# A decode layer's last rows: batch rows 8 partitions apart, and one store for two

## The chip, the cores and the metric

The kernel runs on one core of a Trainium2 chip. The metric is the device time of one execution in microseconds (us), measured on the chip; the median of three runs of the kernel before is 378.41 us (378.24 to 378.53). The profile is of one execution taken by the hardware profiler. PE is TensorE's matmul side and PEld its weight loads, DVE is VectorE, ACT ScalarE, POOL GpSimd, SP SyncE. "SPq" and "ACTq" are the sequencers of those engines, which issue DMAs. L706 is line 706 of the kernel.

## The reference

One layer for one new token in each of four batch rows, D = 576: layernorm, attention over the last 4096 positions of a cache (32 query heads over 16 key/value heads of 128), a projection back to 576, and a feed-forward block with a gated ReLU of width 4608; both with a residual.

```python
def _A_ref(x, k_cache, v_cache, wq, wo):
    W = min(4096, max(256, Sk // 4))                 # Sk = 16384: W = 4096
    q = ((x @ wq).reshape(B, Sq, Hq, Dh)).transpose(0, 2, 1, 3)
    k = jnp.repeat(k_cache[:, :, Sk - W:, :], rep, axis=1)
    v = jnp.repeat(v_cache[:, :, Sk - W:, :], rep, axis=1)
    p = softmax(jnp.einsum("bhqd,bhkd->bhqk", q, k) * (Dh ** -0.5))
    o = jnp.einsum("bhqk,bhkd->bhqd", p, v)
    return o.transpose(0, 2, 1, 3).reshape(B, Sq, Hq * Dh) @ wo

def _B_ref(x, W_gate, W_up, W_down):
    gate = x @ W_gate
    gate = gate * (gate > 0)
    return (gate * (x @ W_up)) @ W_down

h  = x + _A_ref(layernorm(x), k_cache, v_cache, wq, wo)
h2 = h + _B_ref(layernorm(h), W_gate, W_up, W_down)
```

Everything is bf16 in DRAM. The output has 4 rows of 576 values, 4.6 KB. What has to be read is some 160 MB, nearly all of it the K and V windows.

## The kernel before, in words

A small planner (`Prog`) keeps one list of operations for each engine; each names the operations that it depends on. When the lists are written out, each engine waits on the semaphores of what its next operation depends on and then runs it. The order within an engine is the order of the source, and nothing is reordered.

*Loads.* All loads but that of x are issued by SyncE, in one list: wq, then 16 tiles of K and 16 of V of 4 MB each into a ring of four slots (L242), then wo (L266), W_gate and W_up (L276) and W_down in five pieces (L282), cut at rows 0, 15, 25, 32, 35 and 36 of the 36 rows that a partition holds. A load waits only until its place in SBUF has been read for the last time. x is loaded on ScalarE's queue (L335).

*Start.* GpSimd sets the constants (L287 to L329): an identity, masks, zeros. One of them is `sel4`, a 128x32 matrix in fp32 that sums the four groups of 32 partitions into four rows: column b has a one where the partition modulo 32 is b, and the other columns are zero. VectorE finishes some of these constants (L554 to L560), in its list just ahead of the first transposition of K (L422).

*Attention.* For each tile VectorE transposes K in place, PE forms the scores and, four tiles later, the products with V; ScalarE takes the exponentials. This fills the time up to about 340 us.

*Behind attention.* The heads' outputs lie in `oT`, with the four batch rows in columns 0 to 3 of 32. The projection with wo (L607 to L617) runs on the four groups of 32 PE columns side by side, so each group leaves a partial sum of the four rows in the first 4 of its 32 partitions. VectorE and ScalarE copy it out as `part`. Five matmuls (HT, L623; fp32, so PE runs each in two) sum the groups with `sel4` and turn the result round, so that D lies along partitions; residual and layernorm statistics follow (L625 to L643). The normalized rows go to `hnT` (L644, L645), 32 columns per chunk of D, of which columns 0 to 3 hold the batch and the rest are zero.

*Feed-forward.* Gate and up matmuls (L649 to L668) take `hnT` as weights of 32 columns, so that each group of 32 PSUM partitions has the batch in its first 4 rows and zeros in the others. ReLU (L670), product (L673), and a transposition in blocks of 32x32 (L677) give `hhT`, with the batch in columns 0 to 3 of every 32.

*Down projection.* The 576 output columns are cut in two (`ncol`, L681): 272 on PE's columns 0 to 31 and PSUM bank 0, 304 on PE's columns 32 to 63 and bank 1. The two halves of a pass run side by side. Both begin with h: the partial sums `part` through `sel4` (L691), and x through the identity's first 4 rows (L693). 36 passes over W_down's rows follow (L694 to L705); the last has its weights loaded ahead (L697), so only its two matmuls (L34) wait for W_down's last piece.

*Output.* VectorE copies bank 0's half to partitions 0 to 31 of `out_sb` as bf16 (L706), ScalarE bank 1's half to partitions 32 to 63 (L707). The batch rows lie in partitions 0 to 3 and 32 to 35. SyncE stores the first four, ScalarE's queue the second four (L711); both count on the semaphore `d_out`, and SyncE ends by waiting for both (L714, recorded at L110).

Of the kernel before, what the change touches and what calls it, by code (L numbers as in the profile page):

```python
# [6 lines left out]
ALU = mybir.AluOpType  # L7
AX = mybir.AxisListType
FP32 = mybir.dt.float32
BF16 = mybir.dt.bfloat16  # L10

B = 4
# [20 lines left out]
def mm_same(e, out, lhsT, rhs, start, stop, tile, pos):  # L33
    return e.add_instruction(mybir.InstMatmult(  # L34
        name=e.bass.get_next_instruction_name(), engine=mybir.EngineType.PE, ins=[e.lower_ap(rhs), e.lower_ap(lhsT)],
        outs=[e.lower_ap(out)], start_tensor_calc=start, stop_tensor_calc=stop, tile_size=tile, tile_position=pos,
        ldweights=False, bass_skip_group_check=True))
# [83 lines left out]
def bass_sequential_preLN__sliding_block_cached__glu_gated_reglu__decode_kernel(  # L121
# [12 lines left out]
    with ExitStack() as es:  # L134
        cnt = [0]

        def sb(name, shape, dt):
            return es.enter_context(nc.sbuf_tensor("sb_" + name, shape, dt))

        P = Prog()  # L140
        pe = lambda name, fn, deps=(): P.op("tensor", name, fn, deps)
        dve = lambda name, fn, deps=(): P.op("vector", name, fn, deps)
        act = lambda name, fn, deps=(): P.op("scalar", name, fn, deps)
        pool = lambda name, fn, deps=(): P.op("gpsimd", name, fn, deps)
# [6 lines left out]
        ident_b = sb("ident_b", [128, 128], BF16)  # L151
# [6 lines left out]
        c_s4 = o_tmp[:, 512:528].rearrange("p (a b) -> p a b", a=4)  # L158
# [8 lines left out]
        sel4 = sb("sel4", [128, 32], FP32)  # L167
        eps_c = sb("eps_c", [128, 1], FP32)
        warm = sb("warm", [128, 2], FP32)
        x_bf = sb("x_bf", [B, D], BF16)  # L170
# [16 lines left out]
        hnT = sb("hnT", [128, DC + 1, 32], BF16)  # L187
        R_sb = sb("R_sb", [128, DC, 2, B], FP32)
        st2 = sb("st2", [128, 40], FP32)
        tmp5 = sb("tmp5", [128, DC, B], FP32)  # L190
        out_sb = sb("out_sb", [128, 352], BF16)


        pT = pp[:, 0:4096]
# [2 lines left out]
        part = pp[:, 0:1152].bitcast(FP32)  # L197
        partd = pp[:, 1152:1408].bitcast(FP32)
# [7 lines left out]
        bank = [psb[:, i, :] for i in range(8)]  # L206
        bankb = [psb[:, i, :].bitcast(BF16) for i in range(8)]
        ot_ps = bank[6]
        m_ps = bank[7]
# [19 lines left out]
        def ring_slot():  # L229
            s = ring[0] % NSLOT  # L230
            ring[0] += 1
            return s
# [12 lines left out]
        def main_rows(W):  # L245
            return W[0:512, :].rearrange("(p r) n -> p (r n)", r=4)
# [5 lines left out]
        s = ring_slot()  # L252
# [16 lines left out]
        for g, W in ((0, B_W_gate), (1, B_W_up)):  # L269
            for m, n, src in ((4, F // 2, last_rows(W)), (0, 3 * F, main_rows(W)[:, 0:3 * F]), (3, F, main_rows(W)[:, 3 * F:4 * F])):  # L270
                if g == 0 and m == 0:
                    n, src = 4 * F, main_rows(W)
# [7 lines left out]
        for r0, r1 in zip(WD_ROWS, WD_ROWS[1:]):  # L280
            place(("wd", r0), wd_off + r0 * D, (r1 - r0) * D, ("DOWN", 1),
                  lambda e, r0=r0, r1=r1: e.dma_start(  # L282
                      out=arena[:, wd_off + r0 * D:wd_off + r1 * D],
                      in_=B_W_down.rearrange("(p r) n -> p (r n)", p=128)[:, r0 * D:r1 * D]))
# [18 lines left out]
                                                in_=c_qm[:, :, :].rearrange("p q (h j) -> p q h j", j=4),  # L303
# [4 lines left out]
                                                in_=to_v[:, :, :].rearrange("p n (k a) -> p n k a", a=4),  # L308
# [8 lines left out]
        pool("c_s41", lambda e: e.affine_select(out=c_s4[:, :, :], in_=c_s4[:, :, :], pattern=[[-1, 4], [-32, 4]],  # L317
                                                compare_op=ALU.not_equal, fill=1.0, base=0, channel_multiplier=1), ["c_s40"])
        pool("c_sel0", lambda e: e.memset(sel4[:, :], 0.0))
        pool("c_selc0", lambda e: e.memset(selc[:, :, :, :], 0.0))  # L320

        pool("c_toq0", lambda e: e.memset(toq[:, :, :, :], 1.0))
        for sg in range(2):
            pool(f"c_toq{sg + 1}", lambda e, sg=sg: e.affine_select(
                out=toq[:, :, :, :], in_=toq[:, :, :, :],
# [25 lines left out]
        def chunk(t, td, c):  # L351
            return td if c == 4 else t[:, 0:512].rearrange("b (p r) -> b r p", r=4)[:, c, :]
# [186 lines left out]
        def finish_o():  # L539
            for q in range(4):  # L540
                for qd in range(4):
# [11 lines left out]
        put_q()  # L553
        dve("c_qm", lambda e: e.tensor_reduce(out=qm[:, :], in_=c_qm[:, :, :], axis=AX.X, op=ALU.max), ["c_qm1"])  # L554
        dve("c_e8", lambda e: e.tensor_reduce(out=e8[:, :], in_=c_e8[:, :, :], axis=AX.X, op=ALU.max), ["c_e81"])
        dve("c_sel", lambda e: e.tensor_reduce(out=sel4[:, 0:4], in_=c_s4[:, :, :], axis=AX.X, op=ALU.max),
            ["c_s41", "c_sel0"])
        dve("c_selc", lambda e: e.tensor_copy(out=bass.AP(tensor=selc, offset=0, ap=[[128, 128], [33, 4], [4, 8]]),
                                              in_=bass.AP(tensor=e8, offset=0, ap=[[8, 128], [0, 4], [1, 8]])), ["c_e8", "c_selc0"])
        dve("c_toq", lambda e: e.tensor_tensor(out=toq[:, :, :, :], in0=toq[:, :, :, :],  # L560
# [46 lines left out]
        for a in range(8):  # L607
            for n in range(2):
                for j in range(4):
                    out_ = bank[n][32 * j:32 * j + 32, 0:288]  # L610
                    lhsT, rhs = oT[:, 8 * j + a, :], wo[:, 8 * j + a, n * 288:(n + 1) * 288]
                    if n:
                        fn = lambda e, a=a, j=j, out_=out_, lhsT=lhsT, rhs=rhs: mm_same(e, out_, lhsT, rhs, a == 0, a == 7, (128, 32), (0, 32 * j))
                    else:
                        fn = lambda e, a=a, out_=out_, lhsT=lhsT, rhs=rhs: e.matmul(
                            out_, lhsT=lhsT, rhs=rhs, start=(a == 0), stop=(a == 7), skip_group_check=True)
# [3 lines left out]
        dve("partd", lambda e: e.tensor_copy(out=partd.rearrange("p (r a) -> p r a", a=2),  # L620
                                             in_=bass.AP(tensor=psb, offset=512 + 224, ap=[[4096, 128], [1, 64], [0, 2]])), ["part1"])
        for c in range(DC):
            pe("HT", lambda e, c=c: e.matmul(m_ps[:, c * 4:(c + 1) * 4], lhsT=chunk(part, partd, c), rhs=sel4[:, 0:4],  # L623
                                             start=True, stop=True), ["part0", "part1", "partd", "c_sel"] if c == 0 else [])
        dve("h1", lambda e: e.tensor_tensor(out=R_sb[:, :, 0, :], in0=m_ps[:, 0:20].rearrange("p (c b) -> p c b", b=B),  # L625
                                            in1=xT[:, :, :], op=ALU.add), ["HT", "xT"])
# [1 line left out]
        for lo, hi, one in ((0, 4, ones_d), (4, 5, ones_hd)):  # L628
# [4 lines left out]
                                            axis=AX.X, op=ALU.add), ["STAT"])  # L633
# [7 lines left out]
        rstd_bc = bass.AP(tensor=st2, offset=20, ap=[[40, 128], [0, DC], [1, B]])  # L641
        dve("n1", lambda e: e.tensor_tensor(out=tmp5[:, :, :], in0=R_sb[:, :, 0, :], in1=mean_bc, op=ALU.subtract), ["s1"])
        dve("n2a", lambda e: e.tensor_tensor(out=tmp5[:, :, :], in0=tmp5[:, :, :], in1=rstd_bc, op=ALU.mult), ["n1", "s6"])  # L643
        dve("n2", lambda e: e.tensor_copy(out=hnT[:, 0:4, 0:4], in_=tmp5[:, 0:4, :]), ["n2a", "c_hnT"])  # L644
        dve("n3", lambda e: e.tensor_tensor(out=hnT[:, 4:6, 0:4], in0=bass.AP(tensor=tmp5, offset=16, ap=[[20, 128], [0, 2], [1, 4]]),  # L645
                                            in1=bass.AP(tensor=par, offset=0, ap=[[2, 128], [1, 2], [0, 4]]), op=ALU.mult), ["n2a", "c_hnT"])


        for g in range(2):  # L649
            for c in (4, 0, 1, 2, 3):  # L650
                part_ = c if c == 4 or (c == 3 and g) else 0
                for m in range(3):
                    for j in range(4):
# [4 lines left out]
                        lo = gu_off[(g, part_)] + ((c - part_) * F + 1152 * j if c < 4 else 1152 * (j % 2)) + 384 * m  # L658
                        out_, lhsT = bank[3 * g + m][32 * j:32 * j + 32, 0:384], hnT[:, c if c < 4 else 4 + j // 2, :]
# [3 lines left out]
                        else:  # L663
                            fn = lambda e, out_=out_, lhsT=lhsT, lo=lo, c=c: e.matmul(  # L664
                                out_, lhsT=lhsT, rhs=arena[:, lo:lo + 384], start=(c == 4), stop=(c == 3), skip_group_check=True)
# [10 lines left out]
        for i in range(2):  # L676
            dve(("HHT", i), lambda e, i=i: e.transpose(  # L677
                out=hhT[:, 576 * i:576 * i + 576].rearrange("p (r q) -> p r q", q=32),
                in_=bass.AP(tensor=pp, offset=3712 + 18 * i, ap=[[PPW, 128], [1, 18], [36, 32]])), [("HH", m) for m in range(3)])

        ncol = ((0, 272), (272, 576))  # L681

        def down(n, lhsT, w, start, stop, held=False):
            lo, hi = ncol[n]
            out_ = bank[n][32 * n:32 * n + 32, 0:hi - lo]
            if held:
                return lambda e: mm_same(e, out_, lhsT, w[:, lo:hi], start, stop, (128, 32), (0, 32 * n))
            return lambda e: e.matmul(out_, lhsT=lhsT, rhs=w[:, lo:hi], start=start, stop=stop, skip_group_check=True)  # L688
# [1 line left out]
        for n in range(2):  # L690
            pe(None, down(n, sel4[:, :], part, True, False), [("G", 1)])  # L691
        for n in range(2):
            pe(None, down(n, ident_b[0:B, 0:32], x_bf[:, :], False, False))  # L693
        for r in range(36):  # L694
            if r == 35:
                for n in range(2):
# [1 line left out]
            for n in range(2):  # L698
# [4 lines left out]
                    if r % 18 == 0:  # L703
                        deps.append(("HHT", r // 18))
                pe(("DOWN", n), down(n, hhT[:, 32 * r:32 * r + 32], arena[:, wd_off + r * D:wd_off + r * D + D], False, r == 35, r == 35), deps)  # L705
        dve("OUT0", lambda e: e.tensor_copy(out=out_sb[0:32, 0:272], in_=bank[0][0:32, 0:272]), [("DOWN", 0)])  # L706
        act("OUT1", lambda e: e.copy(out=out_sb[32:64, 0:304], in_=bank[1][32:64, 0:304]), [("DOWN", 1)])  # L707
        orow = out.rearrange("b s d -> (b s) d")
        for n in range(2):
            lo, hi = ncol[n]  # L710
            P.dma(("sync", "scalar")[n], ("O", n), lambda e, n=n, lo=lo, hi=hi: e.dma_start(  # L711
                out=orow[:, lo:hi], in_=out_sb[32 * n:32 * n + 4, 0:hi - lo]),
                "d_out", [f"OUT{n}"])
        P.op("sync", None, None, [("O", n) for n in range(2)])  # L714
        P.emit(nc, es)


# [26 lines left out]
```

## Time and profile before

| What | Value |
|---|---|
| Median of 3 runs | 378.41 us (378.24 to 378.53) |
| The profiled execution's own time | 378.4 us |
| Its span, first to last instruction | 377.1 us |
| Around the span | 1.3 us |
| Mean granted TensorE clock | 0.814 |
| Busy: PE, DVE, ACT, POOL | 211.5, 228.6, 53.8, 10.5 us |
| Read from HBM | 159.58 MB, 423 GB/s over the span |
| SyncE's DMA queue (q1) | 98.7% of 16 engines' time |

The page cuts the span into 40 slices of 9.4 us, in which a digit is a busy share in tenths. The chain that ended last is followed back from the last instruction, at each step to what released it. The timeline lists instructions with start and duration in us and, in brackets, how long the engine had been idle before and what ended that. In the DMA part, q1 is the queue that SyncE issues on and q10 ScalarE's; a packet of 4 bytes behind data packets is the write that tells the semaphore of a landing.

### The profile page before, as it was taken

Reading aid. Unit: us, or ns where it says so; the run is one execution under the profiler, and the core shown is the slowest. Engines: PE = TensorE matmul, PEld = TensorE weight load, DVE = VectorE, ACT = ScalarE, POOL = GpSimd, SP = SyncE. Lnnn points to the kernel's source line nnn. Section 1 sums busy time; section 2 is a strip of 40 time slices with the busy share of each in tenths; the row PEclk is TensorE's granted clock in tenths of the full one; section 3 lists DMA queues with packets and bytes.
Section 4 is the critical chain, followed back from the end, with each engine's and each line's share of the span. In section 5 each row is a group of like instructions: output and inputs, shape, how many; then the busy total and the mean of one; then the engine's idle time right before and its main releaser. Section 6 shows DMA issues by size and latency. Waiting matters only on the chain.

```text
span 377.1 us, 2556 instructions
## 1 busy us (share of the span) xinstructions
PE 211.5 (56%) x1462; PEld 40.5 (11%) x694; DVE 228.6 (61%) x164; ACT 53.8 (14%) x84; POOL 10.5 (3%) x29
## 2 busy tenths in 40 slices
PE   0404442239919092749283844664655787776747
PEld 0000000001101010101010101110000101003305
DVE  4088878779292969584747778665749423342140
ACT  3093000211000114010101140101010401121010
POOL 8200000000000000000000000000000000000000
PEclk9999687659978677788778895969596989996688
DMA  8999999999999999999999999999999999999996
GB/s 334 445 445 389 443 445 417 417 445 445 419 414 445 439 440 414 431 441 441 417 422 441 441 417 424 441 434 427 421 441 438 433 424 431 430 422 425 435 416 253
DMA packets 6514, 159.74 MB, mean 424 GB/s; under 512 B 732, under 2 KB 872, under 8 KB 1512
## 3 DMA queue, kind: packets, MB, share of 16 engines
q1 hardware_dynamic: 6488, 159.59, 98.7%
q8 instruction: 8, 0.13, 0.1%
q14 instruction: 2, 0.02, 0.0%
q10 hardware_dynamic: 16, 0.01, 0.0%
HBM read 159.58 MB, written 0.00 MB: 423 GB/s over the span
## 4 chain that ended last, share of the span: by engine, by line
DMA 57%; PE 21%; DVE 20%; issue 0%; ACT 0%; SPq 0%
DMA sb_arena<-in_A_k_cache_dram 48%; DVE sb_arena L422 16%; PE psb L34 13%; DMA sb_arena<-in_B_W_down_dram 9%; PE psb L446 4%; PE psb L507 3%; DVE sb_o_tmp L520 1%; DVE sb_pp L485 1%; PE psb L473 1%; PE psb L688 0%; DVE sb_pp L468 0%; DVE sb_hx L451 0%; ACT sb_pp L465 0%; SPq L282 0%; SPq L255 0%
## 5 line engine op out<-in xcount | busy, mean ns | idle before, releaser
L422 DVE STREAM_TRANSPOSE sb_arena<-sb_arena 128x8192 f32<-128x8192 f32 (+1 forms) x19 | 140.0, 7366 | 67.1 <-DMA sb_arena<-in_A_k_cache_dram 67.1
L446 PE MATMUL psb<-sb_arena 128*32 128x512 bf16 x256 | 44.3, 637 | 119.7 <-DVE sb_arena L422 119.7
L34 PE MATMUL psb<-sb_arena,sb_pp 128*128 128x512 bf16 (+1 forms) x386 | 105.8, 383 | 0.0
L507 PE MATMUL psb<-sb_arena,sb_pp 128*128 128x512 bf16 x128 | 49.6, 388 | 8.9 <-DVE sb_o_tmp L520 8.9
L34 PE MATMUL psb<-sb_arena 128*32 128x512 bf16 x256 | 45.2, 639 | 0.0
L517 ACT COPY sb_o_tmp<-psb 32x512 f32<-32x512 f32 x32 | 18.5, 578 | 179.4 <-PE psb L34 179.1
L520 DVE TENSOR_TENSOR sb_o_tmp<-psb,sb_fm 32x512 f32<-32x512 f32 x32 | 21.7, 678 | 16.9 <-PE psb L34 16.4
L446 PEld LDWEIGHTS psb<-sb_arena 128*32 128x32 bf16 x256 | 10.4, 119 | 161.6 <-DVE sb_arena L422 132.7
L507 PEld LDWEIGHTS psb<-sb_arena,sb_pp 128*128 128x128 bf16 x128 | 12.6, 99 | 113.2 <-issue 113.2
L524 DVE TENSOR_REDUCE sb_o_sel<-sb_o_tmp 128x128 f32<-128x512 f32 x16 | 17.6, 1103 | 0.5
L465 ACT ACTIVATE sb_pp<-psb,sb_hx 128x1024 bf16<-128x1024 f32 x4 | 4.5, 1114 | 79.1 <-DVE sb_hx L462 79.1
L485 DVE TENSOR_TENSOR sb_pp<-psb,sb_m 128x1024 bf16<-128x1024 f32 x8 | 9.4, 1210 | 4.5 <-PE psb L473 4.5
L480 ACT ACTIVATE sb_pp<-psb,sb_m 128x512 bf16<-128x512 f32 x16 | 9.8, 699 | 14.8 <-PE psb L473 14.8
L523 DVE TENSOR_TENSOR sb_o_tmp<-sb_o_tmp,sb_fm 64x512 f32<-64x512 f32 x16 | 11.0, 689 | 0.5
L413 ACT COPY sb_arena<-sb_q_keep 32x256 bf16<-32x256 bf16 x8 | 9.7, 1452 | 0.1
L688 PE MATMUL psb<-sb_arena,sb_pp 128*32 128x272 bf16 (+1 forms) x70 | 6.8, 357 | 4.3 <-DMA sb_arena<-in_B_W_down_dram 4.3
L399 DVE CAST sb_pp<-psb 128x512 bf16<-128x512 f32 x1 | 2.4, 2427 | 10.4 <-PE psb L379 10.4
L468 DVE STREAM_TRANSPOSE sb_pp<-sb_pp 128x1024 bf16<-128x1024 bf16 x4 | 5.0, 1246 | 5.1 <-ACT sb_pp L465 5.1
L473 PE MATMUL psb<-sb_pp,sb_to_v 128*32 128x256 bf16 x64 | 4.3, 402 | 6.2 <-DVE sb_pp L468 6.2
L673 DVE TENSOR_TENSOR sb_pp<-psb,sb_pp 128x384 bf16<-128x384 f32 x3 | 1.5, 551 | 9.0 <-PE psb L664 9.0
L664 PE MATMUL psb<-sb_arena,sb_hnT 128*32 128x384 bf16 x40 | 4.2, 405 | 3.9 <-DVE sb_hnT L645 2.0
L34 PE MATMUL psb<-sb_arena,sb_hnT 128*32 128x384 bf16 x80 | 6.3, 399 | 0.0
(120 smaller groups left out, 85.5 us busy)
## 6 DMA issues: line engine op xcount, KB each, us to landing
sb_arena<-in_A_k_cache_dram SPq DMA_DIRECT2D x16, 4096.0 KB, 26.1
sb_arena<-in_A_v_cache_dram SPq DMA_DIRECT2D x16, 4096.0 KB, 28.5
sb_arena<-in_A_wo_dram SPq DMA_DIRECT2D x1, 4608.0 KB, 26.2
sb_arena<-in_B_W_gate_dram SPq DMA_DIRECT2D x1, 4608.0 KB, 29.3
sb_arena<-in_A_wq_dram SPq DMA_DIRECT2D x1, 4096.0 KB, 12.6
sb_arena<-in_B_W_up_dram SPq DMA_DIRECT2D x1, 3456.0 KB, 30.4
sb_arena<-in_B_W_down_dram SPq DMA_DIRECT2D x1, 2160.0 KB, 29.6
sb_arena<-in_B_W_down_dram SPq DMA_DIRECT2D x1, 1440.0 KB, 32.7
```

The source lines that it names most:

```text
L34: return e.add_instruction(mybir.InstMatmult(name=e.bass.get_next_instruction_name(), engine=mybir.EngineType.PE, ins=[e.lower_ap(rhs), e. ...
L413: act("QW", lambda e, i=i, q=q: e.copy(out=bass.AP(tensor=arena, offset=32 * i * AW + 2 * i + q, ap=[[AW, 32], [512, 16], [136, 4], [32, 4]]),
L422: dve(("TRA", g), lambda e: e.transpose(out=dst, in_=src), [("L", "K", g)] if lo == 0 else [])
L446: fn = lambda e, out_=out_, lhsT=lhsT, rhs=rhs, start=start, stop=stop: e.matmul(out_, lhsT=lhsT, rhs=rhs, start=start, stop=stop, skip_gr ...
L473: pe(("RM", b, n // 2), lambda e, n=n, i=i: e.matmul(bank[6 if n < 2 else 0][32 * i:32 * i + 32, n % 2 * 256:n % 2 * 256 + 256], lhsT=to_v ...
L480: act(("EV", b, 0), lambda e, a=a: e.activation(out=bass.AP(tensor=pp, offset=2 * a, ap=[[PPW, 128], [8, 2], [32, 128], [1, 2]]), in_=bank ...
L485: dve(("EV", b, 1), lambda e, n=n: e.tensor_tensor(out=bass.AP(tensor=pp, offset=16 + 8 * n, ap=[[PPW, 128], [32, 128], [2, 4], [1, 2]]), ...
L507: fn = lambda e, lhsT=lhsT, rhs=rhs, k=k, j=j: e.matmul(bank[2 + j], lhsT=lhsT, rhs=rhs, start=(k == 0), stop=(k == 7), skip_group_check=True)
L517: act(("OSC", g), lambda e, j=j: e.copy(out=o_tmp[32 * j:32 * j + 32, 0:512], in_=bank[2 + j][32 * j:32 * j + 32, :]), [("PV", g), ("OSEL" ...
L520: dve(("OSD", g), lambda e, j=j: e.tensor_tensor(out=ot(32 * j, 32), in0=bank[2 + j][32 * j:32 * j + 32, :].rearrange("p (t d) -> p t d", ...
L523: dve(("OS", g), lambda e: e.tensor_tensor(out=ot(64, 64), in0=ot(64, 64), in1=fmb(64, 64), op=ALU.mult), [("OSC", g)])
L524: dve(("OSEL", g), lambda e: e.tensor_reduce(out=o_sel[:, qd, b, :], in_=o_tmp[:, 0:512].rearrange("p (t d) -> p d t", d=DH), axis=AX.X, o ...
```

## The change

From the feed-forward on, the four batch rows are not put next to each other but 8 partitions apart: 0, 8, 16 and 24 of each group of 32. To this end the ones of `sel4` go to columns 0, 8, 16 and 24; HT reads these four columns; the normalized rows are written to these columns of `hnT`; and x enters the down projection through `id8`, a 4x32 matrix with ones in those columns (a memset on GpSimd and a copy on VectorE at the start), in place of the identity's first rows. The 32x32 transposition keeps the places.

The output columns are cut in two equal halves of 288 where they were 272 and 304. Both evictions write 288 columns, to partitions 0 to 31 and 32 to 63 of `out_sb`. One DMA on SyncE's queue takes every eighth of these 64 partitions, eight rows of 576 bytes, and writes them to DRAM as 2 halves x 4 rows. It waits for both evictions. ScalarE issues no store.

```diff
-        out_sb = sb("out_sb", [128, 352], BF16)
+        out_sb = sb("out_sb", [64, 288], BF16)
+        id8 = sb("id8", [B, 32], BF16)
...
+        pool("c_id80", lambda e: e.memset(id8[:, :], 0.0))
...
-        dve("c_sel", lambda e: e.tensor_reduce(out=sel4[:, 0:4], in_=c_s4[:, :, :], axis=AX.X, op=ALU.max),
+        dve("c_sel", lambda e: e.tensor_reduce(out=sel4[:, 0:32:8], in_=c_s4[:, :, :], axis=AX.X, op=ALU.max),
             ["c_s41", "c_sel0"])
+        dve("c_id8", lambda e: e.tensor_copy(out=id8[:, 0:32:8], in_=ident_b[0:B, 0:B]), ["c_idb", "c_id80"])
...
-            pe("HT", lambda e, c=c: e.matmul(m_ps[:, c * 4:(c + 1) * 4], lhsT=chunk(part, partd, c), rhs=sel4[:, 0:4],
+            pe("HT", lambda e, c=c: e.matmul(m_ps[:, c * 4:(c + 1) * 4], lhsT=chunk(part, partd, c), rhs=sel4[:, 0:32:8],
...
-        dve("n2", lambda e: e.tensor_copy(out=hnT[:, 0:4, 0:4], in_=tmp5[:, 0:4, :]), ["n2a", "c_hnT"])
-        dve("n3", lambda e: e.tensor_tensor(out=hnT[:, 4:6, 0:4], in0=bass.AP(tensor=tmp5, offset=16, ap=[[20, 128], [0, 2], [1, 4]]),
+        dve("n2", lambda e: e.tensor_copy(out=hnT[:, 0:4, 0:32:8], in_=tmp5[:, 0:4, :]), ["n2a", "c_hnT"])
+        dve("n3", lambda e: e.tensor_tensor(out=hnT[:, 4:6, 0:32:8], in0=bass.AP(tensor=tmp5, offset=16, ap=[[20, 128], [0, 2], [1, 4]]),
...
-        ncol = ((0, 272), (272, 576))
+        ncol = ((0, 288), (288, 576))
...
-            pe(None, down(n, ident_b[0:B, 0:32], x_bf[:, :], False, False))
+            pe(None, down(n, id8[:, :], x_bf[:, :], False, False), ["c_id8"])
...
-        dve("OUT0", lambda e: e.tensor_copy(out=out_sb[0:32, 0:272], in_=bank[0][0:32, 0:272]), [("DOWN", 0)])
-        act("OUT1", lambda e: e.copy(out=out_sb[32:64, 0:304], in_=bank[1][32:64, 0:304]), [("DOWN", 1)])
-        orow = out.rearrange("b s d -> (b s) d")
-        for n in range(2):
-            lo, hi = ncol[n]
-            P.dma(("sync", "scalar")[n], ("O", n), lambda e, n=n, lo=lo, hi=hi: e.dma_start(
-                out=orow[:, lo:hi], in_=out_sb[32 * n:32 * n + 4, 0:hi - lo]),
-                "d_out", [f"OUT{n}"])
-        P.op("sync", None, None, [("O", n) for n in range(2)])
+        dve("OUT0", lambda e: e.tensor_copy(out=out_sb[0:32, :], in_=bank[0][0:32, 0:288]), [("DOWN", 0)])
+        act("OUT1", lambda e: e.copy(out=out_sb[32:64, :], in_=bank[1][32:64, 0:288]), [("DOWN", 1)])
+        P.dma("sync", "O", lambda e: e.dma_start(out=out.rearrange("b s (n c) -> n (b s) c", n=2),
+                                                 in_=bass.AP(tensor=out_sb, offset=0, ap=[[8 * 288, 8], [1, 288]])), "d_out", ["OUT0", "OUT1"])
+        P.op("sync", None, None, ["O"])
```

## The prediction

> **What bounds the kernel now.** I read the page first: span, slices, queues.
>
> ```profile
> span 377.1 us, 2556 instructions
> ...
> DMA  8999999999999999999999999999999999999996
> ...
> q1 hardware_dynamic: 6488, 159.59, 98.7%
> ...
> q10 hardware_dynamic: 16, 0.01, 0.0%
> ```
>
> SyncE's queue (q1) takes 98.7% of the 16 DMA engines' time over the span, with 159.6 MB of cache and weights. No load is altered by the change, so it can move only what lies behind the stream (the last slice, a 6), unless it disturbs the stream itself. Then the chain that ended last, in order of time (start, us, what), for the last 46 us:
>
> ```profile
> 338.79 34.63 DMA sb_arena<-in_B_W_down_dram
> 373.42 0.04 issue
> 373.46 1.62 PE psb L688 x20
> 375.08 0.14 PE psb L34 x2
> 375.23 0.02 issue
> 375.25 0.40 ACT sb_out_sb L707
> ```
>
> The W_down loads decide until 373.42; then come the last passes of the down projection and one eviction. What follows the eviction the timeline and the DMA view of the end show:
>
> ```profile
> 374.88 0.33 PE L34 MATMUL psb<-sb_arena,sb_pp 128*32 128x272 bf16 x2
> 375.20 0.43 DVE L706 CAST sb_out_sb<-psb 32x272 bf16<-32x272 f32 x1 [8.30 <-PE psb L34]
> 375.25 0.40 ACT L707 CAST sb_out_sb<-psb 32x304 bf16<-32x304 f32 x1 [15.49 <-PE psb L34]
> 375.65 0.33 SPq L711 DMA_DIRECT2D out_dram<-sb_out_sb  x1
> 375.68 0.27 ACTq L711 DMA_DIRECT2D out_dram<-sb_out_sb  x1
> ```
>
> ```profile
> GB/s 0 0 0 0 0 0 0 0 0 0 0 0 0 0 0 0 0 0 0 0 0 13 27 27 27 14 0 0 0 0 0 0 0 0 0 0 0 0 0 0
> DMA packets 16, 0.00 MB, mean 3 GB/s; under 512 B 8, under 2 KB 16, under 8 KB 16
> ```
>
> The second fence is the stretch 375.5 to 377.2 in 40 slices of 0.0425 us. Bytes move only in slices 22 to 26, that is for 0.20 us from about 376.42 on. The trace's packet records say the same: eight data packets of 26 to 31 ns (four of 544 B, four of 608 B), begun 20 to 28 ns after each other from 376.42 to 376.59, each followed by a packet of 4 bytes that tells of its landing. The semaphore's records show these eight landings from 376.78 to 377.11, 0.33 to 0.49 us after their packets (mean 0.40). SyncE's last wait ends at 377.13, the span at 377.14. So from the later issue to the end it is 377.14 - 375.68 = 1.46 us, of which the bytes take 0.20.
>
> **The change part by part.**
>
> Start: one memset more on GpSimd (4x32 bf16) and one copy more on VectorE (id8). The nearest rows are the memset of 128x32 at L319, 0.13 us, and the reduce and copy at L556 and L558, 0.15 and 0.20 us. GpSimd's list is over at 12.2 us and its results are first wanted at 22.2. Behind the copy in VectorE's queue is the first transposition of K, for which the engine idles:
>
> ```profile
> 22.34 0.29 DVE L560 TENSOR_TENSOR sb_toq<-sb_toq,sb_par 128x128 f32<-128x128 f32 x1
> 23.68 8.71 DVE L422 STREAM_TRANSPOSE sb_arena<-sb_arena 128x8192 f32<-128x8192 f32 x1 [1.05 <-DMA sb_arena<-in_A_k_cache_dram]
> ```
>
> 0.20 us fits into 1.05: cost 0, and 0.20 at most were that cover gone. No DMA is issued earlier or later.
>
> Middle: L556, L644 and L645 write with a step of 8 elements, and HT's ten matmuls (2.25 us together) read four columns with that step. The counts of elements stay (16 and 8 per partition). I bound the price by doubling: +0.17 and +0.16 for L644 and L645, +2.25 for HT, below by 0. They precede the gate and up matmuls, which afterwards wait for W_up (0.78 and 1.14 us) and then 3.71 us for W_down's first part at 367.63. Of the doubled price, 2.58 us, the two waits for W_up take 1.92; the 0.66 left would delay the multiply at L673 and the transposes behind it, which end at 366.90 and are wanted at 367.63. So even that is covered: cost 0; without the cover of W_up, 1.85 us at most would reach the down projection.
>
> Down projection: the two column groups run side by side, and at the full clock a pass of 304 columns takes 0.129 us and one of 272 takes 0.116 (spacing of their starts). 288 columns by the line between: 0.1225. Up to 374.25 this hides behind W_down's next landing (the passes restart at 373.46 and 374.52). Behind that, three steps count: the last 304-column pass now starts at 374.92; with 288, both start at 374.52 + 0.133 (between the first spacings after the restart, 0.126 and 0.140) + 2 x 0.1225 = 374.90 and last 0.284 (between 0.277 and 0.292), so both halves are ready at 375.18 (now 375.16 and 375.21).
>
> Evictions: VectorE's takes 0.43 for 272 columns, and the 288-column copy at L618 0.46 (fp32 out); I take 0.45. ScalarE's 288 at L619 took 0.40; I take 0.39 against 0.40 for 304. They start 0.04 after PE: VectorE ends at 375.18 + 0.04 + 0.45 = 375.67, ScalarE at 375.61. SyncE now waits for both; nothing is queued behind this wait but its own last one. It issues 0.02 after the later, at 375.69 instead of 375.65 and 375.68. Against the later of today: +0.01.
>
> The store: ScalarE's DMA and its 0.27 us issue go; they ran beside SyncE's, so that is worth 0. The new one has two levels of rows on the DRAM side (2 x 4), where the old ones had one. A row for that:
>
> ```profile
> L242 SPq DMA_DIRECT2D sb_arena<-in_A_v_cache_dram x16: 534/535/536, 46.2 to 297.9; - x16
> ...
> L266 SPq DMA_DIRECT2D sb_arena<-in_A_wo_dram x1: 336/336/336, 311.5 to 311.5; - x1
> ```
>
> K and V loads (two levels in DRAM) take SyncE 0.535 us to issue, the one-level load of wo after a wait 0.336, the old store 0.332. So issuing costs 0.20 more; whether the bytes start later by that no row shows, as all those loads stand behind others. Bounds: 0 and +0.20. I take +0.20, for the first packet came 0.44 and 0.52 us after the two stores' issues had ended.
>
> The bytes: eight rows now start over 0.17 us. Whether that is one engine after another, or the place of the rows, the trace can't say; bounds: all at once (0.03) and one after another as now (0.19). I take 0.10, about the middle, which is also what two runs of four rows beside each other, at the measured 24 ns, would give. Landing: 0.33 to 0.49 us; I take the mean of the eight, 0.40, as fewer landings have to be waited for.
>
> Sum: 375.69 + 0.332 + 0.20 + 0.44 = 376.66 first packet; + 0.10 = 376.76; + 0.40 = 377.16; + 0.03 to the end = 377.19, against 377.14: +0.05 us. The profiled execution took 378.4 for its span of 377.1, with 1.3 around it, and equals the median of 378.41. Forecast: 378.45.
> With all lower bounds the end is at 375.69 + 0.77 + 0.03 + 0.33 + 0.03 = 376.85 (-0.29), with all upper ones 376.66 + 0.19 + 0.49 + 0.03 = 377.37 (+0.23).
>
> A rule to weigh here: today's four rows per store went with four packets of 4 bytes per queue, so each row had its own ring. The Trainium skill, "DMA: Bandwidth & Descriptors", section "Why a DMA increments its semaphore by 16 and not by 1", says that the engines used are the largest number up to 16 that divides the outermost counts of both sides. For 4 and 4 that is 4, as the trace has it; for 8 and 2 it would be 2, so the one store would get fewer engines than either of the two, which speaks against the change. By it, four rows follow each other on each of two engines, 0.10 us and the same sum; eight free engines would give 0.03 and 378.38.
> "SBUF — State Buffer", section "Door 1: The DMA port swizzle", puts partitions 0 to 3 and 32 to 35 on one port and rows 8 apart on four. If the port is why the rows now go one by one, spreading them saves up to 0.16 of the 0.19, and the sum is 378.4 instead of 378.45. No run here shows which.
>
> **The rivals.**
> *Nothing that can be told* is the forecast itself: a measurement here can tell about 0.2% (0.76 us) from no change, and my bounds are -0.29 and +0.23. For it: the whole path behind the last eviction is 1.46 us.
>
> *Faster*: the spread rows and the single landing count shorten the store. Worked out with the lower bounds: 378.1. To pass 0.2% it would have to take away half of the 1.46 us, though 0.33 is issue, 0.44 the gap to the first packet and 0.33 the quickest landing. Only the unmeasured 1.3 us around the span could give the rest (a queue less to close). Against it: q10 is still used for x.
>
> *Slower*: the store with two levels and rows 8 partitions apart starts as slowly as the other small DMA of the trace, the load of x (four rows, issued at 0.94, 0.54 us to issue, first used at 3.34): 2.40 us from issue to use, against 377.13 - 375.68 = 1.45. Price +0.95: 379.4. It decides from a path of 1.45 + 0.75 = 2.2 us on. Against it: x ran cold and between loads at 334 GB/s, the store runs on idle engines.
>
> *The stream is disturbed*: a loss of 0.2% of its rate (423 GB/s) is 0.76 us by itself, at any place. For it: q1 has no slack. Against it: not one load's issue, order or size changes.
>
> **How the numbers follow.** The forecast's case (378.0 to 378.75: bounds of -0.29 and +0.23 about 378.4, and 0.1 on each side, for the runs shown lie 0.17 below to 0.12 above the median) 0.80; store as slow as x 0.07; stream slower 0.06, at 379.2 and more; faster by over 0.2%, from the stream or from around the span, 0.07. So faster 0.07, within 0.80, slower 0.13. The range 378.0 to 378.9 takes in the first case and the near edge of the slower ones.
>
> **What would show it.** SyncE's issue of the store at about 0.53 us (0.33 if I am wrong); 288-column evictions ending at 375.67 and 375.61 in the timeline, relative to the last pass; eight data packets whose window in the DMA view shrinks from 0.20 to about 0.12 us, and fewer landings than eight; the wait of SyncE's last instruction 1.1 us as now or up to 0.2 more. The prediction is wrong if that wait grows beyond 1.9 us, if VectorE's first transposition starts later than K's landing, or if the W_down landings move by more than 0.5 us.

## The result, and the profile after

The changed kernel takes 378.83 us (median of 22 runs, 378.40 to 379.19), the kernel before 378.31 us in as many runs (377.91 to 378.64). The ratio is 1.0015, with a 95% interval of 1.0009 to 1.0021. So the change costs 0.5 us, or 0.15%: within the 0.2% that was set as the limit of what can be told, but 22 runs do tell it. The profiled execution took 379.09 us for a span of 377.6 us.

The page's slices and queues, as before, show the stream as it was; q10 has lost the store and keeps only the load of x:

```profile
span 377.6 us, 2543 instructions
...
DMA  8999999999999999999999999999999999999995
...
q1 hardware_dynamic: 6490, 159.59, 98.7%
...
q10 hardware_dynamic: 8, 0.00, 0.0%
```

The end of the chain that ended last (start, us, what). VectorE's eviction has taken the place of ScalarE's: both halves are now ready together, and VectorE's copy is the longer one (0.45 us against 0.39):

```profile
374.63 0.55 PE psb L691 x6
375.18 0.16 PE psb L34 x2
375.34 0.44 DVE sb_out_sb L709
```

The timeline of the same end, and below it the DMA view of 375.5 to 377.7 us in 40 slices of 0.055 us:

```profile
375.01 0.29 PE L34 MATMUL psb<-sb_arena,sb_pp 128*32 128x288 bf16 x2
375.33 0.45 DVE L709 CAST sb_out_sb<-psb 32x288 bf16<-32x288 f32 x1 [8.44 <-PE psb L34]
375.36 0.39 ACT L710 CAST sb_out_sb<-psb 32x288 bf16<-32x288 f32 x1 [14.99 <-PE psb L34]
375.84 0.67 SPq L711 DMA_DIRECT2D out_dram<-sb_out_sb  x1
```

```profile
GB/s 0 0 0 0 0 0 0 0 0 0 0 0 0 0 0 0 0 0 0 0 0 0 0 0 0 0 0 0 0 31 42 11 0 0 0 0 0 0 0 0
DMA packets 10, 0.00 MB, mean 2 GB/s; under 512 B 2, under 2 KB 10, under 8 KB 10
```

The evictions end at 375.78 and 375.75. The store's issue begins at 375.84 and lasts 0.67 us, where the two stores had 0.33 and 0.27. Its first packet comes at 377.11, 1.27 us after the issue began (0.77 and 0.79 before). Eight rows and two landings follow, where eight landings followed. From the issue to the end of the span it is 1.77 us, from the two issues before 1.49 and 1.46.

That is not all of it. The time of a run less its span is a second place:

| | Span, us | Around the span, us |
|---|---|---|
| Changed, median of 22 runs | 377.3 | 1.50 (1.45 to 1.56) |
| Before, 33 runs beside the first experiments | 376.7 | 1.27 |

The kernel before has 1.26 to 1.27 us around the span in every group of runs, so its span was about 378.31 - 1.27 = 377.04 in the 22 runs compared. Of the 0.52 us, then, some 0.23 lie outside the instructions that the profile shows, and 0.29 inside.

### The profile page after: what moved, and what is told of

It is laid out like the page before. It is cut to its first block, busy times and chain, and to the rows that moved or that the text cites. A ratio compares the mean times of both kernels' runs of the same rounds, so it can differ in the third digit from the quotient of the medians.

```text
span 377.6 us, 2543 instructions
## 1 busy us (share of the span) xinstructions
PE 209.1 (55%) x1447; PEld 38.7 (10%) x694; DVE 229.0 (61%) x165; ACT 53.7 (14%) x84; POOL 10.6 (3%) x30
## 4 chain that ended last, share of the span: by engine, by line
DMA 62%; DVE 18%; PE 18%; SPq 1%; issue 1%
DMA sb_arena<-in_A_k_cache_dram 53%; DVE sb_arena L424 16%; PE psb L34 11%; DMA sb_arena<-in_B_W_down_dram 9%; PE psb L448 4%; PE psb L509 3%; DVE sb_o_tmp L522 1%; DVE sb_pp L487 1%; SPq L243 0%; SPq L283 0%; PE psb L475 0%; PE psb L691 0%; DVE sb_out_sb L709 0%; SPq L256 0%; SPq L252 0%
## 5 line engine op out<-in xcount | busy, mean ns | idle before, releaser
L34 PE MATMUL psb<-sb_arena,sb_pp 128*128 128x512 bf16 x384 | 107.3, 388 | 2.8 <-issue 2.6
L509 PE MATMUL psb<-sb_arena,sb_pp 128*128 128x512 bf16 x115 | 44.6, 388 | 9.0 <-DVE sb_o_tmp L522 9.0
L691 PE MATMUL psb<-sb_arena,sb_pp 128*32 128x288 bf16 x70 | 6.9, 367 | 4.4 <-DMA sb_arena<-in_B_W_down_dram 4.3
L34 PE MATMUL psb<-sb_arena,sb_hnT 128*32 128x384 bf16 x80 | 6.3, 398 | 0.0
L453 DVE TENSOR_REDUCE sb_hx<-psb 128x1 f32<-128x1024 f32 x4 | 4.9, 1225 | 2.1 <-PE psb L34 2.1
```

What stands on the lines that cost most here:

```text
L34: return e.add_instruction(mybir.InstMatmult(name=e.bass.get_next_instruction_name(), engine=mybir.EngineType.PE, ins=[e.lower_ap(rhs), e. ...
L509: fn = lambda e, lhsT=lhsT, rhs=rhs, k=k, j=j: e.matmul(bank[2 + j], lhsT=lhsT, rhs=rhs, start=(k == 0), stop=(k == 7), skip_group_check=True)
```

## The experiments

The table compares each kernel with the kernel before on the same chip (33 runs of it in each group, 11 of each experiment). "Path" is the time from the start of the store's issue (the first, where there are two) to the end of the span, in the profiled execution; "first packet" counts from the same issue.

| Kernel | Time; before it (us) | Ratio, 95% interval | Issue, us | First packet | Path | Around the span |
|---|---|---|---|---|---|---|
| two_stores | 378.92; 377.98 | 1.0024, 1.0015 to 1.0033 | 0.70, 0.75 | 1.35 | 2.16 | 1.49 |
| one_level | 378.63; 377.98 | 1.0017, 1.0008 to 1.0025 | 0.72 | 1.33 | 1.79 | 1.50 |
| full_rows | 378.65; 377.98 | 1.0017, 1.0008 to 1.0026 | 0.75 | 1.36 | 1.85 | 1.48 |
| four_outer | 378.58; 377.98 | 1.0015, 1.0006 to 1.0024 | 0.72 | 1.33 | 1.79 | 1.49 |
| adjacent_parts | 378.28; 378.13 | 1.0006, 0.9997 to 1.0015 | 0.27, 0.33 | 0.76 | 1.41 | 1.47 |
| before_spread | 378.77; 378.13 | 1.0017, 1.0008 to 1.0026 | 0.75, 0.70 | 1.35 | 2.09 | 1.28 |
| full_adjacent | 378.24; 378.13 | 1.0004, 0.9995 to 1.0013 | 0.35 | 0.78 | 1.33 | 1.27 |
| one_level_again | 378.42; 378.13 | 1.0006, 0.9997 to 1.0014 | 0.35 | 0.80 | 1.27 | 1.49 |
| before_id8 | 378.28; 378.03 | 1.0008, 0.9999 to 1.0017 | 0.33, 0.27 | 0.77 | 1.49 | 1.49 |
| before_pool | 378.13; 378.03 | 1.0002, 0.9994 to 1.0011 | 0.34, 0.28 | 0.77 | 1.49 | 1.26 |
| step_two | 378.74; 378.03 | 1.0019, 1.0010 to 1.0027 | 0.79 | 1.40 | 1.86 | 1.50 |
| two_levels_adjacent | 378.67; 378.03 | 1.0019, 1.0010 to 1.0028 | 0.78 | 1.38 | 1.88 | 1.48 |

**two_stores: the new layout with two stores again.**

```diff
-        P.dma("sync", "O", lambda e: e.dma_start(out=out.rearrange("b s (n c) -> n (b s) c", n=2),
-                                                 in_=bass.AP(tensor=out_sb, offset=0, ap=[[8 * 288, 8], [1, 288]])), "d_out", ["OUT0", "OUT1"])
+        for n in range(2):
+            P.dma(("sync", "scalar")[n], ("O", n), lambda e, n=n: e.dma_start(
+                out=orow[:, 288 * n:288 * n + 288], in_=bass.AP(tensor=out_sb, offset=32 * n * 288, ap=[[8 * 288, 4], [1, 288]])),
+                "d_out", [f"OUT{n}"])
```

> The changed kernel with the rows 8 partitions apart and the equal halves kept, but with two stores again, the left half on SyncE's queue and the right half on ScalarE's, each with 4 rows and one level of rows in DRAM. Theory A (the single store with two levels in DRAM takes SyncE 0.67 us to issue instead of 0.33 and sends its first packet 0.5 us later): issues of about 0.33 and 0.27 us, issue to end about 1.46 us, span near 377.1, time as the kernel before within 0.1 us (378.3). Theory B (the spacing of 8 partitions, id8 or the layout of the feed-forward costs the 0.5 us): time stays at 378.8, with issue to end near 1.75 us or with an earlier stage late. On the window of the packets: if the rows' place decides, eight packets overlap and take about 0.1 us; if not, 0.2 us as before.

Its timeline and its DMA view (375.5 to 377.7 us):

```profile
375.45 0.70 ACTq L713 DMA_DIRECT2D out_dram<-sb_out_sb  x1
375.48 0.75 SPq L713 DMA_DIRECT2D out_dram<-sb_out_sb  x1
```

```profile
GB/s 0 0 0 0 0 0 0 0 0 0 0 0 0 0 0 0 0 0 0 0 0 0 0 21 21 0 0 0 0 0 32 11 0 0 0 0 0 0 0 0
```

Theory A does not explain this: these stores have one level in DRAM, and each takes as long to issue as the changed kernel's, or longer. (That two levels are free as well does not follow; two_levels_adjacent, below, shows that they are not.) Nor do the two run beside each other. ScalarE's four rows move at 376.80, SyncE's at 377.15, in two lumps. Two stores of this kind are worse than one: 378.92 us here and 378.63 in one_level, next to the same runs of the kernel before, with ranges that do not meet (378.80 to 379.10, 378.47 to 378.78). The single store does save something, but out of a loss that the layout brought in.

**one_level, full_rows and four_outer: one store, other destinations.** The first writes eight rows one after the other, the second four whole rows.

```diff
-        P.dma("sync", "O", lambda e: e.dma_start(out=out.rearrange("b s (n c) -> n (b s) c", n=2),
+        P.dma("sync", "O", lambda e: e.dma_start(out=out.rearrange("b s (n c) -> (b s n) c", n=2),
```

> The changed kernel's single store of the same eight partitions, written to DRAM as eight rows of 576 bytes one after the other (one level). The halves land in another order than the reference's. Theory A (levels in DRAM): issue back to about 0.33 us, first packet 0.77 us after the issue's start instead of 1.27, issue to end about 1.3 us, time 378.3 or less. Theory B (spacing of partitions on the SBUF side): issue stays near 0.67 us, time 378.8. Theory C (number of engines used: two in the changed kernel): eight landings instead of two; if few engines cost the time, the gain shows in the packets' window and in the landings, not in the issue.

```diff
-        dve("OUT0", lambda e: e.tensor_copy(out=out_sb[0:32, :], in_=bank[0][0:32, 0:288]), [("DOWN", 0)])
-        act("OUT1", lambda e: e.copy(out=out_sb[32:64, :], in_=bank[1][32:64, 0:288]), [("DOWN", 1)])
+        dve("OUT0", lambda e: e.tensor_copy(out=out_sb[:, 0:288], in_=bank[0][0:32, 0:288]), [("DOWN", 0)])
+        act("OUT1", lambda e: e.copy(out=out_sb[:, 288:576], in_=bank[1][32:64, 0:288]), [("DOWN", 1)])
...
+        P.dma("sync", "O", lambda e: e.dma_start(out=out.rearrange("b s d -> (b s) d"),
+                                                 in_=bass.AP(tensor=out_sb, offset=0, ap=[[8 * 576, 4], [1, 576]])), "d_out", ["OUT0", "OUT1"])
```

> The changed kernel with both evictions written to the same 32 partitions (columns 0 to 287 and 288 to 575) and one store of 4 rows of 1152 bytes, one level on both sides, 8 partitions apart. Theory A: issue about 0.33 us, first packet 0.77 us after its start, four packets of about 51 ns, issue to end about 1.35 us from 375.73 on relative to a last landing of W_down at 374.84: span near 377.1, time 378.2 to 378.4. Theory B (spacing): 378.8. If a single store without ScalarE's costs time around the span (1.48 us in the changed kernel's profiled run, 1.26 in the one before), that 0.2 us stays here and the time is 378.5.

```diff
-        P.dma("sync", "O", lambda e: e.dma_start(out=out.rearrange("b s (n c) -> n (b s) c", n=2),
-                                                 in_=bass.AP(tensor=out_sb, offset=0, ap=[[8 * 288, 8], [1, 288]])), "d_out", ["OUT0", "OUT1"])
+        P.dma("sync", "O", lambda e: e.dma_start(out=out.rearrange("b s (n c) -> (b s) n c", n=2)[:, :, 0:272],
+                                                 in_=bass.AP(tensor=out_sb, offset=0, ap=[[8 * 288, 8], [1, 272]])), "d_out", ["OUT0", "OUT1"])
```

> One store of the same eight partitions with two levels in DRAM, but 4 outside and 2 inside (the changed kernel has 2 outside and 4 inside), and only the first 272 columns of each half, so that the levels do not merge. It leaves out 16 columns of each half and writes the halves in another order. Theory A (two levels cost): issue near 0.6 us or more and the time of the changed kernel, 378.8, with four landings. Theory C (two engines with four rows each cost): four engines take two rows each, issue to end falls from 1.75 towards 1.5 us, time 378.5.

The issues of one_level and of full_rows:

```profile
375.51 0.72 SPq L711 DMA_DIRECT2D out_dram<-sb_out_sb  x1
```

```profile
375.47 0.75 SPq L711 DMA_DIRECT2D out_dram<-sb_out_sb  x1
```

Both are as slow as the changed kernel's, with one level and with eight or four landings in place of two. So neither the levels nor the number of engines is what made these two slow, and theory B, the step of 8 partitions, remains. four_outer turned out not to test what it was meant to: its rows lie 576 bytes apart all through, so they went out as one level of eight, as the eight landings in its DMA view say:

```profile
DMA packets 16, 0.00 MB, mean 2 GB/s; under 512 B 8, under 2 KB 16, under 8 KB 16
```

It is a second one_level with rows of 544 bytes, and gives the same path, 1.79 us.

**adjacent_parts and before_spread: the step alone, taken away and put in.**

```diff
-                out=orow[:, 288 * n:288 * n + 288], in_=bass.AP(tensor=out_sb, offset=32 * n * 288, ap=[[8 * 288, 4], [1, 288]])),
+                out=orow[:, 288 * n:288 * n + 288], in_=bass.AP(tensor=out_sb, offset=32 * n * 288, ap=[[288, 4], [1, 288]])),
```

> The kernel of two_stores with one number changed: both stores read four adjacent partitions (0 to 3, 32 to 35) instead of every eighth. The stored rows are not the batch rows then, but sizes and destinations are the same; feed-forward, id8, equal halves stay as changed. Theory B1 (a step of 8 partitions on the SBUF side of a store costs about 0.4 us of issue, and 0.2 us around the span): issues fall from 0.75 and 0.70 to 0.33 and 0.27 us, what lies around the span from 1.50 to 1.27 us, time to 378.0. Theory B2 (the layout of the feed-forward or id8 costs): time stays at 378.9 and the issues at 0.7 us.

```diff
-                out=orow[:, lo:hi], in_=out_sb[32 * n:32 * n + 4, 0:hi - lo]),
+                out=orow[:, lo:hi], in_=bass.AP(tensor=out_sb, offset=32 * n * 352, ap=[[8 * 352, 4], [1, hi - lo]])),
```

> The kernel before with one number changed: both stores read every eighth partition. The batch rows lie in adjacent partitions there, so of each store's rows only the first is the reference's; everything else is as before. Theory B1: issues rise to about 0.75 and 0.70 us, what lies around the span from 1.27 to 1.50 us, time from 378.0 to 378.9; the packets of a store overlap. Theory B2: time stays at 378.0.

The two issues of adjacent_parts, and then those of before_spread:

```profile
375.37 0.27 ACTq L713 DMA_DIRECT2D out_dram<-sb_out_sb  x1
375.39 0.33 SPq L713 DMA_DIRECT2D out_dram<-sb_out_sb  x1
```

```profile
375.30 0.75 SPq L711 DMA_DIRECT2D out_dram<-sb_out_sb  x1
375.33 0.70 ACTq L711 DMA_DIRECT2D out_dram<-sb_out_sb  x1
```

Their bytes, in the same order, in slices of 0.055 us from 375.5 us on:

```profile
GB/s 0 0 0 0 0 0 0 0 0 0 0 21 21 21 21 0 0 0 0 0 0 0 0 0 0 0 0 0 0 0 0 0 0 0 0 0 0 0 0 0
GB/s 0 0 0 0 0 0 0 0 0 0 0 0 0 0 0 0 0 0 0 0 0 30 10 0 0 0 33 11 0 0 0 0 0 0 0 0 0 0 0 0
```

One number in the source, the step, moves each issue by 0.42 to 0.43 us and the first packet by 0.6. The feed-forward's new layout is all in adjacent_parts, and its span (mean 376.85 us) is that of the kernel before (376.88): inside the span the layout costs nothing that 11 runs can tell, with a store whose path is 0.08 us shorter (1.41 against 1.49). before_spread has the old layout and a span of 377.57, 0.69 us more. Theory B1 holds for the issue and falls for the rest: the 0.2 us around the span does not go with the step. It is there in adjacent_parts (1.47) and absent in before_spread (1.28).

**full_adjacent and one_level_again: one store without the step.** The first is the kernel before with one store of four whole rows, the second is one_level with adjacent partitions.

```diff
-        ncol = ((0, 272), (272, 576))
+        ncol = ((0, 288), (288, 576))
...
+        act("OUT1", lambda e: e.copy(out=out_sb[0:32, 288:576], in_=bank[1][32:64, 0:288]), [("DOWN", 1)])
+        P.dma("sync", "O", lambda e: e.dma_start(out=out.rearrange("b s d -> (b s) d"), in_=out_sb[0:4, :]), "d_out", ["OUT0", "OUT1"])
```

> The kernel before with equal halves, both evicted to the same 32 partitions, and one store of 4 adjacent partitions of 1152 bytes on SyncE's queue: one store without the spacing. Theory B1: issue about 0.33 us; against the kernel before SyncE waits for two engines (+0.06 us) and has four landings to wait for, not eight (-0.1 us); time 377.9 to 378.1, with 1.27 us around the span. If a single store, or a ScalarE without one, costs by itself, time 378.2 to 378.6.

```diff
-                                                 in_=bass.AP(tensor=out_sb, offset=0, ap=[[8 * 288, 8], [1, 288]])), "d_out", ["OUT0", "OUT1"])
+                                                 in_=bass.AP(tensor=out_sb, offset=0, ap=[[288, 8], [1, 288]])), "d_out", ["OUT0", "OUT1"])
```

> The kernel of one_level with the step of 8 partitions set to 1: eight adjacent partitions, eight rows of 576 bytes, one level, eight landings. The stored rows are not the batch rows. Theory B1: issue 0.72 to 0.33 us, first packet 0.77 us after its start instead of 1.33, what lies around the span 1.27 us, time 378.63 less 0.6 to 0.8, thus 377.9 to 378.0. If eight rows or the wait for two engines cost, the issue stays at 0.7 us.

The issue of full_adjacent, then that of one_level_again:

```profile
375.40 0.35 SPq L708 DMA_DIRECT2D out_dram<-sb_out_sb  x1
```

```profile
375.56 0.35 SPq L711 DMA_DIRECT2D out_dram<-sb_out_sb  x1
```

A single store for SyncE costs nothing by itself: the paths are 1.33 and 1.27 us, against 1.49 with two stores. In the whole time that gain isn't seen: full_adjacent is at 1.0004 of the kernel before, with an interval that holds 1. It waits 0.03 us longer to issue, as SyncE waits for two engines in turn, and 0.1 us is below what 11 runs tell. It is the nearest to a better version, and no faster than the kernel before. one_level_again came out at 378.42, 0.4 to 0.5 us above its forecast of 377.9 to 378.0. It kept the 1.49 us around the span, which is 0.22 of that; another 0.15 is the comparison, as the kernel before was itself at 378.13 beside these runs and at 377.98 beside those of one_level, from which the forecast was reckoned. What is left is within what 11 runs can tell.

**before_id8 and before_pool: what lies around the span.**

```diff
+        id8 = sb("id8", [B, 32], BF16)
...
+        pool("c_id80", lambda e: e.memset(id8[:, :], 0.0))
...
+        dve("c_id8", lambda e: e.tensor_copy(out=id8[:, 0:32:8], in_=ident_b[0:B, 0:B]), ["c_idb", "c_id80"])
```

> The kernel before, with only the two start instructions of the change added (the memset on GpSimd and the copy on VectorE that make id8), whose result nothing reads. In all kernels so far that have them, what lies around the span is 1.47 to 1.50 us, in those without 1.27. Theory D (these two instructions lengthen what lies around the span, though inside the span they are hidden): around the span 1.49 us, span as before, time +0.22 us. Rival (something else of the changed layout does it): 1.27 us and no change in the time.

before_pool has the first two of these three lines:

> The kernel before with the GpSimd memset of id8 alone. Theory D with GpSimd's instruction as the cause: around the span 1.49 us, time +0.22 us. With VectorE's copy as the cause: 1.27 us, time as before.

With both instructions the time around the span is 1.49 us (1.43 to 1.54 over 11 runs), with the memset alone 1.26 (1.20 to 1.32), in the kernel before 1.26. The ranges do not touch, though the two whole times, 378.28 and 378.13, have intervals that do. So the copy on VectorE, which takes 0.15 us inside the span and is hidden there, adds 0.23 us outside. What happens in it the profile does not show, and whether it is this copy or any further instruction on VectorE wasn't tried.

**step_two and two_levels_adjacent: what makes a store slow.**

```diff
-                                                 in_=bass.AP(tensor=out_sb, offset=0, ap=[[288, 8], [1, 288]])), "d_out", ["OUT0", "OUT1"])
+                                                 in_=bass.AP(tensor=out_sb, offset=0, ap=[[2 * 288, 8], [1, 288]])), "d_out", ["OUT0", "OUT1"])
```

> The kernel of one_level_again (eight rows, one level, eight landings) with every second partition instead of adjacent ones; the stored rows are not the batch rows. Theory B1 in the form that any step over 1 costs: issue 0.72 us and first packet 1.33 us after its start, as with a step of 8; time about 0.55 us over one_level_again. In the form that only far steps cost (rows in different groups of 4 partitions): issue between 0.35 and 0.7 us, rising with the number of groups (4 groups here, 8 with a step of 8, 2 with a step of 1).

In two_levels_adjacent the changed kernel's step of `8 * 288` is `288`, and the two levels in DRAM stay.

> The changed kernel's store word for word, two levels in DRAM and two landings, but from eight adjacent partitions; the stored rows are not the batch rows. If two levels in DRAM cost nothing (with a step of 8 the store of two levels took 0.67 us to issue, that of one level 0.72): issue 0.35 us, first packet 0.8 us after its start, time as one_level_again. If they cost what the loads of K and V show: issue 0.53 us, first packet about 1.0 us, time 0.2 us over one_level_again.

The issue of step_two, then that of two_levels_adjacent:

```profile
375.42 0.79 SPq L711 DMA_DIRECT2D out_dram<-sb_out_sb  x1
```

```profile
375.20 0.78 SPq L711 DMA_DIRECT2D out_dram<-sb_out_sb  x1
```

A step of 2 costs what a step of 8 costs, so it is not a matter of distance. And two levels in DRAM cost the same even from adjacent partitions: 0.78 us of issue and 1.38 to the first packet. Both paths are 0.6 us longer than one_level_again's; against the kernel before, the two whole times are 0.71 and 0.64 us longer, one_level_again's 0.29. That one_level was no quicker than the changed kernel did not mean that levels are free. The two causes do not add: the changed kernel has both and its issue is the shortest of the slow ones, 0.67. The store is of the quick kind only where it takes adjacent partitions and has one level in DRAM. Why stays open. In the loads a second level goes with 0.20 us of issue (0.535 against 0.336), in the store with 0.42 (0.78 against 0.35); whether that is the direction of the transfer, or that each of these kernels ends with the only stores of the slow kind that it has, so that a second one on the same engine might be quicker, wasn't tried.

## Why the prediction was right or wrong

The range (378.0 to 378.9) holds the 378.83, and "within 0.2%" came true, but partly by luck. The forecast was 378.45, a loss of 0.05 us, and the sum's own upper bound was a loss of 0.23; the loss is 0.52. 378.83 lies above the 378.75 at which the forecast's case ends, in the strip that was added for a slower stream or a store as slow as the load of x, and neither of these came at its price. And the kernel before ran 0.10 us faster in these runs (378.31) than in the three that the forecast starts from (378.41); on top of those, the same loss would have given 378.93, outside the range. Point by point:

- *Start.* Hidden inside the span, as written. After the change VectorE still waits for K:

```profile
21.58 0.15 DVE L560 COPY sb_id<-sb_ident_b 4x4 bf16<-4x4 bf16 x1
...
23.75 8.71 DVE L424 STREAM_TRANSPOSE sb_arena<-sb_arena 128x8192 f32<-128x8192 f32 x1 [1.75 <-DMA sb_arena<-in_A_k_cache_dram]
```

  "Cost 0, and 0.20 at most were that cover gone" was wrong all the same: the copy costs 0.23 us, outside the span. The prediction took the 1.3 us around the span for a constant, and it isn't one. In the case "faster" it was named as an unmeasured place; as a place for a loss it wasn't thought of.
- *Middle.* Right: the product behind the gate and up matmuls starts at 362.99 and the transposes behind it at 364.51 in both traces, and with all of the layout in place adjacent_parts' span is as before.
- *Down projection and evictions.* Right: both halves start their last pass together (375.01), and the evictions take 0.445 and 0.390 us for the 0.45 and 0.39 forecast.
- *Wait for both evictions.* The issue was put 0.02 us behind the later eviction and came 0.065 behind it. SyncE waits for the two engines in two instructions; the first is a recorded wait of its own: 0.04 us.
- *The store's issue.* The mechanism was there, the size was not: +0.20, from the K and V loads with two levels, measured +0.33; two levels alone, from adjacent partitions, make it +0.45 (0.78). That the step between partitions alone does it too (0.72) was nowhere in the sum: for that spacing only the packets' place was weighed. Nor was +0.20 the upper bound of the prediction's own rows: it says 0.535 us for the K loads too, but the longest of the 16 took 0.69 (the first three, issued 0.04 us after one another, took 0.61 to 0.69), 0.36 more than the old store.
- *From the issue's end to the first packet.* 0.44 was carried over from the old store; measured 0.60. With the issue, the first packet is 0.50 us later than the old one's, where 0.20 was taken as the upper bound. This is the term that failed, and the bound with it.
- *Bytes and landing.* Right: the eight rows start over 0.10 us (forecast 0.10), and landings take 0.34 to 0.35 us behind their packets (forecast 0.40). By the Trainium skill, "DMA: Bandwidth & Descriptors", section "Why a DMA increments its semaphore by 16 and not by 1", an outermost 8 and 2 would give two engines. The two landings here, eight in one_level (8 and 8) and four in full_rows (4 and 4) agree. But behind the first packet two engines took 0.50 us to the end and eight (one_level) 0.47: the rule was right and hardly mattered.
- *The place of the rows.* The Trainium skill, "SBUF — State Buffer", section "Door 1: The DMA port swizzle", puts partitions 0 to 3 on one port and rows 8 apart on several. Four rows of 1152 bytes took 0.18 us from adjacent partitions (full_adjacent) and 0.12 from spaced ones (full_rows), which agrees with it; rows of 576 bytes show no gain, eight of them taking about 0.09 us either way (one_level_again, one_level) and four as well (adjacent_parts, two_stores). So spacing gained 0.06 us in the packets at best, against some 0.55 that it costs before the first of them.
- *The rivals.* "Slower" had the right place, a store that starts late; its price, from the load of x, was +0.95, and it came to +0.28 to 0.31 on the path. "The stream is disturbed" is not seen: W_down's last landing came at 374.93 us against 374.84, and in the experiments it lies anywhere from 374.27 to 374.89 without going with an edit.
- *The signs.* The issue was to show it at 0.53 us, and at 0.67 did. The other sign, SyncE's last wait at 1.1 us or up to 0.2 more, came true at 1.1 and hid the loss: behind the issue's end it is 0.16 us longer to the first packet, but 0.22 shorter from there to the end (0.50 against 0.72).

The sum of the two profiled executions, from the later eviction's end on: 0.035 for the second wait (0.065 against 0.030), 0.53 from the later issue to the first packet (1.27 against 0.74), -0.07 for the bytes, -0.155 for the last landing (0.34 behind its packet against 0.49), in all 0.34; the evictions end 0.04 later against W_down's last landing (0.85 against 0.81), a phase that varies from 0.81 to 0.85 over the runs. Over many runs the spans differ by about 0.29, and 0.23 around the span make it the 0.52 of the medians.

## What to carry to other kernels

The small store at the very end of this kernel is nearly all latency (the changed one's bytes take 0.13 of its 1.77 us), and the shape of its access moved that latency by half a microsecond: before rows are rearranged so that fewer or better spread packets go out, read from a trace what the issue and the time to the first packet are for a store of exactly that shape. Time outside the span belongs to the sum as well: compare "time less span" of the two kernels over several runs, for here an instruction hidden inside the span (0.15 us) was paid for outside (0.23).

## What the runs showed of the hardware

- A store of 2 to 5 KB from adjacent partitions with one level in DRAM took 0.27 to 0.35 us to issue, and 0.76 to 0.80 us from the issue's start to the first packet (of the first store, where there are two). With a step of 2 or 8 partitions, or with two levels in DRAM, it was 0.67 to 0.79 us and 1.27 to 1.40 us. One of the two is enough, and both together are no worse.
- Two stores of the slow kind, issued 0.02 to 0.03 us apart on SyncE and ScalarE, did not overlap: first packets at 376.80 and 377.15 (two_stores), 376.66 and 376.93 (before_spread). Two of the quick kind got all their rows out within 0.20 us: in the kernel before they began 0.05 us apart and alternate, in adjacent_parts the second began 0.10 us behind the first, just after its last row.
- In the ten kernels with one copy more on VectorE at the start the time around the span was 1.47 to 1.50 us on the mean, in the four without it 1.26 to 1.28; before_id8 (1.49) and before_pool (1.26) differ in this copy alone.
